# An output projection in 128-row tiles, fourteen products for fifteen, and four steps that move with it

## The chip, the core and the metric

The kernel runs on one core of a Trainium2 chip. A core has five engines with a queue of instructions each: TensorE (matrix products; PE in the profile, PEld its weight loads), VectorE (DVE), ScalarE (ACT), GpSimd (POOL) and SyncE (SP), which here issues every DMA. An engine works through its queue in order, and an instruction that waits holds up all behind it. The metric is device time in microseconds, lower is better.

## The reference

Two branches read the same normalized input and are multiplied. S = 2048 rows, D = 576 columns, H = 32 heads of 18 columns, F = 4608 hidden columns, all in fp32.

```python
xn  = layernorm(x)
qkv = xn @ wqkv                                  # three of 32 heads x 18
p   = softmax(einsum("bhqd,bhkd->bhqk", q, k) * 18 ** -0.5)
s   = einsum("bhqk,bhkd->bhqd", p, v).reshape(S, D) @ wo
g   = silu((gelu(xn @ w_gate) * (xn @ w_up)) @ w_down)
out = x + s * g
```

The change touches the product with `wo`, and the last line.

## The kernel before

**Split operands.** Where a product has to be more exact than one pass of TensorE's fp32r format, each operand is split into a high part (the value rounded to fp32r) and a low part (the rest), and three products are summed in PSUM: high with high, high with low, low with high. `split` does it on POOL (lines 93 to 96: one instruction for the high part, one for the low), `split_av` on ACT and VectorE, `split_ap` on ACT and POOL.

**The stages.** A prologue (lines 138 to 349) normalizes x, transposes it and makes q, k and v, all of which go to DRAM. It also splits `wo` into rows of `wos` in DRAM (`split_wo`, `store_wo`). Then the gated network (FFN) and the attention run together. The FFN is cut into 144 sections: each computes 128 hidden columns for a block of 512 rows (`section`, 54 matmuls into pg and pu), and its activation runs on ACT and VectorE (`activate`, lines 379 to 394) with one buffer t1, which `finish` then splits into hh and hl. After every second section four groups of six products go through w_down (`down`, py), and VectorE adds them to Y (line 412). The weights of a section are split by POOL in three chunks (wh, wl: five buffers each).

Nine sections come before the attention proper (`FIRST`, lines 756 to 773). They carry the first score products whose row maxima VectorE takes (`max_mm`, line 654). When one unit's maxima are complete, `max_neg` negates and splits them (three VectorE instructions), `max_end` transposes them with a matmul (line 667) and a DMA writes them beside q as extra rows. Then 128 sections (lines 774 to 795) run with the attention of 32 units, a unit being four heads and 512 rows: scores, Exp on ACT, and the product with v into acc. Seven sections close the FFN (lines 811 to 823), and lines 826 to 853 are the end.

**The output projection.** A unit's output goes to DRAM (oT), its sums' reciprocals too (rT). For each block of 512 rows, tiles of seven heads (126 rows; the fifth has four heads, 72 rows) are loaded into OT, with rT spread over a head's 18 rows in den (`load_o`, two DMAs a tile). `norm_o` multiplies them on POOL. den has one buffer. For each of eight groups of a block (128 rows × 288 columns) `split_o` splits OT into oh and ol on POOL, and `project_o` sums 15 products in PSUM (line 550). In the first three blocks VectorE multiplies by the gate (line 552), POOL adds x (line 553) and a DMA writes the rows. In the last block six groups are kept in S2 until the FFN is done. Then `gate` (ACT's Tanh and a VectorE instruction, line 377), a VectorE product (line 847) and POOL's addition of x (`put`, line 835) follow for each of them; the last two groups are projected at the very end (lines 849 to 853) and added on VectorE.

**What sets the order.** TensorE's instructions run in the order of the code. The other queues are ordered by a planner before the run: it takes the earliest ready instruction in the code's order, so that an instruction can come ahead of its place where its queue has room. `keep_in_program_order` holds single ones in place. `at(n, part, ...)` hangs a step to a part of section n, counted from the first attention section. Tiles of a later stage lie where tiles of the prologue were, and wait for them one by one. OT, with its zero fill on POOL (line 490), lies over the prologue's vn tiles; the KS tiles, whose fills of ones are shared by VectorE and POOL (line 605), lie over other tiles.

Of the kernel before, what the change touches and what calls it, by code (L numbers as in the profile page):

```python
# [17 lines left out]
P = 128  # L18
NT = S // P
TB = 512  # L20
# [20 lines left out]
FIRST = (0, 0, 4, 6, 6, 6, 6, 6, 6)  # L41
ATT = range(len(FIRST), len(FIRST) + NU * NA)
MROW = 3 * DH
HO = 7
KO = HO * DH
NK = -(-D // KO)
EPS = 1e-5
GC = 0.044715
GS = 0.7978845608028654
# [18 lines left out]
def kernel(ctx: ExitStack, tc: tile.TileContext, x, wqkv, wo, w_gate, w_up, w_down, out):  # L68
# [69 lines left out]
    with tc.tile_pool(name="pro", bufs=1) as pro, tc.tile_pool(name="pps", bufs=1, space=PSUM) as pps:  # L138
# [140 lines left out]
            nc.sync.dma_start(vs[t * P:(t + 1) * P, c * H // 2:(c + 1) * H // 2, :], v)  # L279

        def split_wo(k):
            n = min(KO, D - k * KO)
            raw = raw_tile([KO, D])
            tc.keep_in_program_order(nc.sync.dma_start(raw[0:n], wo[k * KO:k * KO + n, :]))
            hi, lo = (pro.tile([KO, D], F32R, name=f"wo{i}", tag="rawp", bufs=5) for i in range(2))
            split(hi[0:n], lo[0:n], raw[0:n])
            return k, n, hi, lo

        def store_wo(k, n, hi, lo):
            for i, t in enumerate((hi, lo)):  # L290
                tc.keep_in_program_order(nc.sync.dma_start(wos[i, k * KO:k * KO + n, :], f(t)[0:n]))

        NQT = 2 * D // P
        def after(what, before):
# [101 lines left out]
    def down(b, r, hs, wd, Y, js):  # L396
        for j in js:
            tt = slice(j * P, (j + 1) * P)
            for c in range(2):
                cc = slice(288 * c, 288 * c + 288)  # L400
                py = ps.tile([P, 288], F32, name="py", tag="s", bufs=2)
                n = 0
                for g in range(G):
                    hh, hl = hs[g]
                    for a, w in ((hh, wd[0]), (hh, wd[1]), (hl, wd[0])):
                        nc.tensor.matmul(py, a[:, tt], w[:, g, cc], start=(n == 0), stop=(n == 3 * G - 1))  # L406
                        n += 1
                yy = Y[:, j, cc]
                if r == 0:
                    nc.vector.tensor_copy(yy, py)  # L410
                else:
                    nc.vector.tensor_tensor(yy, py, yy, op=ALU.add)  # L412
# [73 lines left out]


    op = ctx.enter_context(tc.tile_pool(name="op", bufs=1, reuse_waits="tile"))
    OT = op.tile([KO, NK, TB], F32, name="OT")
    nc.gpsimd.memset(OT, 0.0)  # L490
# [12 lines left out]

    def norm_o(k):
        n, den = OG.pop(("den", k))
        nc.gpsimd.tensor_tensor(OT[0:n, k, :], OT[0:n, k, :], den[0:n], op=ALU.mult)
# [33 lines left out]
    def project_o(b, i, S2=None, o=None):  # L540
        c, j = divmod(i, TB // P)
        cc = place(b, i)[1]
        if b < NB - 1:
            xx, yy = OG["xy"]
        po = ps.tile([P, TB], F32, name="po", tag="m", bufs=3)
        o = o or OG["o"]
        terms = [(k, x, w) for k in range(NK) for x, w in ((0, 0), (0, 1), (1, 0))]
        for m, (k, x, w) in enumerate(terms):
            n = min(KO, D - k * KO)
            nc.tensor.matmul(po[:, 0:288], o[x][0:n, k, :], OW[w][0:n, k, :], start=(m == 0), stop=(m == len(terms) - 1))  # L550
        if b < NB - 1:
            nc.vector.scalar_tensor_tensor(yy, yy, 0.25, po[:, 0:288], op0=ALU.mult, op1=ALU.mult)
            nc.gpsimd.tensor_tensor(yy, yy, xx, op=ALU.add)
            OG["y", b, i] = yy
        elif S2 is not None:
            nc.scalar.activation(S2[:, j, cc], po[:, 0:288], AF.Copy)
        return po[:, 0:288]
# [13 lines left out]
            t()  # L571

    S2 = [None]
    for b in range(NB):
        last = b == NB - 1
        for k in range(NK):
            t0 = b * AB + max(-(-min(H, (k + 1) * HO) // QD) * NA + 3, 22 + 3 * k)
            if not (last and k == NK - 1):
                at(t0, 0, load_o, b, k)
                at(t0 + 2 - last, 2, norm_o, k)  # L580
        first = (b + 1) * AB + 1 if last else max((b + 1) * AB + 6, (b + 1) * NR * G - len(FIRST) + 3)
        if not last:
            first += (first + len(FIRST)) % G
# [16 lines left out]
    with tc.tile_pool(name="att", bufs=1, reuse_waits="tile") as att:  # L600
# [173 lines left out]
        for n in range(NU * NA):  # L774
# [23 lines left out]
    with tc.tile_pool(name="epi", bufs=1, reuse_waits="tile") as epi:  # L798
        S2[0] = epi.tile([P, TB // P, D], F32, name="S2")
        XX = epi.tile([P, TB // P, D], F32, name="XX")  # L800
        n = NU * NA
        todo[n, 2].insert(0, lambda: norm_o(NK - 1))
        def cut(hi, lo, raw):
            split_av(hi, lo, raw, tc.keep_in_program_order)

# [33 lines left out]
        for Y, j, c in finals:  # L839
            cc = slice(288 * c, 288 * c + 288)  # L840
            th = epi.tile([P, 288], F32, name="thl", bufs=len(finals))
            ss = S2[0][:, j, cc]
            gate(th, th, Y[:, j, cc])
            if c * (TB // P) + j > HIND:
                late[c * (TB // P) + j] = th, ss, j, cc
            else:
                nc.vector.scalar_tensor_tensor(ss, th, 0.25, ss, op0=ALU.mult, op1=ALU.mult)
# [34 lines left out]
```

## Time and profile before

| what | value |
|---|---|
| median of three runs | 2657.7 us (2654.64 to 2658.63) |
| profiled execution, own time | 2656.42 us |
| span of its instructions | 2654.6 us |
| mean granted TensorE clock | 0.998 of full |
| busy: PE, PEld, DVE, ACT, POOL | 99%, 77%, 75%, 57%, 52% |
| products of the output projection (line 550) | 480 (384 of 126 rows, 96 of 72 rows) |
| DMA issues of OT and den | 20 and 20 |

An instruction line of a timeline reads: start in us, duration in us, engine, source line, operation, written tile, read tiles, shapes, and in brackets the idle time before it with what ended it. Lines of a list by groups give the count (x128), busy us, mean ns of one, and idle time before with the releasers. A line of the stages has, for a stretch of time, its length, the busy time and the count of each engine, and last the granted clock, the busy share of the DMA engines and GB/s. Matmuls overlap in the record: the time that one costs is its distance from the next one's start.

### The profile page before, as it was taken

How to read it: one execution, taken by the hardware profiler on the slowest of the kernel's cores; microseconds unless marked ns; L12 is line 12 of the kernel's file. 1: busy time of each engine (PE TensorE's matmuls, PEld its weight loads, DVE VectorE, ACT ScalarE, POOL GpSimd, SP SyncE). 2: the span in 40 equal slices, each digit the busy share in tenths (PEclk: the TensorE clock that was granted, in tenths of full speed). 3: DMA queues.
4: the chain of work that ended last, by engine and by line, in shares of the span. 5: the costliest groups of instructions: out<-in, count | busy, mean ns of one | idle time of the engine just before them, and what ended most of it. 6: DMA issues, size and time to landing. Idle time of an engine off the chain costs nothing.

```text
span 2654.6 us, 55995 instructions
## 1 busy us (share of the span) xinstructions
PE 2639.3 (99%) x21032; PEld 2050.3 (77%) x21032; DVE 1999.4 (75%) x3440; ACT 1506.3 (57%) x2690; POOL 1392.4 (52%) x1488
## 2 busy tenths in 40 slices
PE   9999999999999999999999999999999999999999
PEld 8887777777777777777777777777777777777788
DVE  5327888888887888777888887778888877788445
ACT  3222466666666666555666665556666655566632
POOL 2126544545466555555447655555446755555564
PEclk9999999999999999999999999999999999999999
DMA  8875433334355434444346444435335444444341
GB/s 259 267 239 140 114 99 102 97 103 103 96 126 135 106 99 107 122 114 120 103 110 146 124 102 106 119 101 134 102 100 126 134 115 122 108 111 119 77 108 60
DMA packets 390874, 323.66 MB, mean 122 GB/s; under 512 B 105736, under 2 KB 305928, under 8 KB 390604
## 3 DMA queue, kind: packets, MB, share of 16 engines
q1 hardware_dynamic: 390604, 320.08, 45.3%
q8 instruction: 167, 2.74, 0.5%
q14 instruction: 103, 0.84, 0.1%
HBM read 266.58 MB, written 52.85 MB: 120 GB/s over the span
## 4 chain that ended last, share of the span: by engine, by line
PE 97%; POOL 1%; DVE 1%; DMA 0%; issue 0%; ACT 0%; SPq 0%; POOLq 0%; DVEq 0%
PE pg L369 27%; PE py L406 18%; PE acc L718 17%; PE pe L684 10%; PE pm L653 9%; PE pu L369 7%; PE po L159 7%; PE po L550 2%; PE po L212 0%; PE pt L221 0%; POOL wl L95 0%; PE pm L667 0%; DMA den<-rT 0%; DVE thl L377 0%; DMA vs<-vn 0%
## 5 line engine op out<-in xcount | busy, mean ns | idle before, releaser
L685 ACT ACTIVATE pT<-pe 128x512 f32<-128x512 f32 x2048 | 1165.2, 598 | 703.7 <-PE pm L653 533.5
L654 DVE TENSOR_REDUCE mx<-pm 128x1 f32<-128x512 f32 x2048 | 1289.1, 684 | 52.8 <-PE pm L653 32.2
L369 PE MATMUL pg<-xd,wh 64*128 64x512 f32 x2592 | 949.3, 398 | 0.5 <-issue 0.5
L369 PE MATMUL pu<-xd,wh 64*128 64x512 f32 x2592 | 948.9, 398 | 0.0
L684 PE MATMUL pe<-q,KS 56*128 56x512 f32 x2048 | 816.9, 406 | 0.0
L653 PE MATMUL pm<-KS,q 54*128 54x512 f32 x2048 | 796.5, 395 | 4.0 <-DVE mx L654 4.0
L369 PEld LDWEIGHTS pg<-xd,wh 64*128 64x128 f32 x2592 | 483.5, 187 | 66.3 <-issue 31.8
L94 POOL TENSOR_SCALAR wh<-raw 128x384 fp32r<-128x384 f32 x432 | 226.6, 525 | 557.0 <-PE pu L369 336.7
L369 PE MATMUL pg<-xd,wl 64*128 64x512 f32 x1296 | 508.1, 392 | 0.4 <-POOL wl L95 0.4
L369 PE MATMUL pu<-xd,wl 64*128 64x512 f32 x1296 | 508.0, 392 | 0.0
L369 PEld LDWEIGHTS pu<-xd,wh 64*128 64x128 f32 x2592 | 484.4, 187 | 6.2 <-DVE t L387 0.2
L718 PE MATMUL acc<-pT,VS 128*32 128x512 f32 x4096 | 466.0, 595 | 0.0
L95 POOL TENSOR_TENSOR wl<-raw,wh 128x384 fp32r<-128x384 f32 x432 | 440.5, 1021 | 34.3
L684 PEld LDWEIGHTS pe<-q,KS 56*128 56x128 f32 x2048 | 370.6, 184 | 80.9 <-ACT pT L685 20.5
L653 PEld LDWEIGHTS pm<-KS,q 54*128 54x128 f32 x2048 | 377.0, 185 | 30.1 <-DVE mx L654 6.4
L412 DVE TENSOR_TENSOR Y<-py,Y 128x288 f32<-128x288 f32 x544 | 248.4, 457 | 188.6 <-PE py L406 187.6
L406 PE MATMUL py<-dh,hh 128*128 128x288 f32 x1152 | 352.8, 306 | 1.8 <-DVE Y L410 1.6
L406 PE MATMUL py<-dl,hh 128*128 128x288 f32 x1152 | 339.6, 295 | 0.0
L406 PE MATMUL py<-dh,hl 128*128 128x288 f32 x1152 | 338.6, 294 | 0.0
L718 PEld LDWEIGHTS acc<-pT,VS 128*32 128x32 f32 x4096 | 120.3, 109 | 276.8 <-issue 265.0
L369 PEld LDWEIGHTS pg<-xd,wl 64*128 64x128 f32 x1296 | 242.5, 187 | 18.7 <-POOL wl L95 0.8
L406 PEld LDWEIGHTS py<-dh,hh 128*128 128x128 f32 x1152 | 215.8, 187 | 44.4 <-issue 37.7
(118 smaller groups left out, 2929.6 us busy)
## 6 DMA issues: line engine op xcount, KB each, us to landing
KS<-qk SPq DMA_DIRECT2D x1536, 36.0 KB
raw<-in_B_w_gate_dram SPq DMA_DIRECT2D x144, 288.0 KB
raw<-in_B_w_up_dram SPq DMA_DIRECT2D x144, 288.0 KB
raw<-in_B_w_down_dram SPq DMA_DIRECT2D x68, 576.0 KB
VS<-vs SPq DMA_DIRECT2D x128, 152.0 KB
qk<-t SPq DMA_DIRECT2D x72, 256.0 KB
q<-qk SPq DMA_DIRECT2D x384, 36.0 KB
xd<-xhs SPq DMA_DIRECT2D x24, 384.0 KB
```

Of the source, the lines that this page charges most:

```text
L94: first = nc.gpsimd.tensor_scalar(hi, raw, 1.0, 1.0, op0=ALU.mult, op1=ALU.mult)
L95: nc.gpsimd.tensor_tensor(lo, raw, f(hi), op=ALU.subtract)
L159: nc.tensor.matmul(o, st, m, start=(i == 0), stop=(i == len(TERMS) - 1))
L369: nc.tensor.matmul(o, w[1 + wp][k][rr, c, :], xd[xp][k][rr, c, :], start=(i == 0), stop=(i == len(terms) - 1))
L406: nc.tensor.matmul(py, a[:, tt], w[:, g, cc], start=(n == 0), stop=(n == 3 * G - 1))
L412: nc.vector.tensor_tensor(yy, py, yy, op=ALU.add)
L550: nc.tensor.matmul(po[:, 0:288], o[x][0:n, k, :], OW[w][0:n, k, :], start=(m == 0), stop=(m == len(terms) - 1))
L653: nc.tensor.matmul(pm, QS[u, r][rr, t * P:(t + 1) * P], KS[(u * NA + c) % KB][r][rr, :], start=True, stop=True)
L654: nc.vector.tensor_reduce(MX[u][:, 2 * r + a, t, c:c + 1], pm, axis=AX.X, op=ALU.max)
L684: nc.tensor.matmul(pe, KS[(u * NA + c) % KB][r][rr, t * P:(t + 1) * P], QS[u, r][rr, :], start=True, stop=True)
L685: nc.scalar.activation(PT[u, kt][:, 2 * r + a, :], pe, AF.Exp, scale=SCALE)
L718: nc.tensor.matmul(ACC[u][32 * a:32 * a + 32, :], VS[(u * NA + c) % VB][:, v:v + 32], pt[:, a, :], start=(kt == 0), stop=(kt == NT - 1), s ...
```

## The change

The 576 rows of `wo` and of OT are now cut by 128: four tiles and a fifth of 64 rows. The low part of the fifth tile is copied under its high part (`oh` rows 64 to 127, a POOL copy in `split_o`), and `woh` holds the fifth tile's rows twice, `wol` once with zeros under it. Two products of full height then do what three did, and a group has fourteen. Heads straddle tiles, so `load_o` issues a DMA for each run of whole heads or part of a head: 13 for OT and 13 for den in a block. The tiles woh and wol are allocated once.

Four things move. The zero fill of OT, with that of wol's last rows, stands in the code at attention section 4 and no longer ahead of the KS fills. `max_neg` of the first unit comes before the activation of its section and no longer after. The normalizations of tiles 3 and 4 come one section after their loads; in the last block tile 3 is loaded in two parts (heads up to 27, and head 28 after the last unit), and both tiles are normalized after it. In the last `down` the second half of the columns takes its PSUM buffers from the tag "f", so that py has four buffers and not two. At the end VectorE and no longer POOL adds x for the six groups.

```diff
-HO = 7
-KO = HO * DH
-NK = -(-D // KO)
+NK = KT + 1
...
-                py = ps.tile([P, 288], F32, name="py", tag="s", bufs=2)
+                py = ps.tile([P, 288], F32, name="py", tag="sf"[c if b == NB - 1 and r == NR - 1 else 0], bufs=2)
...
-    OT = op.tile([KO, NK, TB], F32, name="OT")
-    nc.gpsimd.memset(OT, 0.0)
-    OW, OG = {}, {}
-
-    def load_o(b, k, pool=op):
-
-        h0, h1 = k * HO, min(H, (k + 1) * HO)
-        n = (h1 - h0) * DH
+    OT = op.tile([P, NK, TB], F32, name="OT")
+    OW = [op.tile([P, NK, 288], F32R, name=name) for name in ("woh", "wol")]
+    OG = {}
+
+    def load_o(b, k, pool=op, heads=range(H)):
+
         toks = slice(b * TB, (b + 1) * TB)
-        den = pool.tile([KO, TB], F32, name="den")
-        nc.sync.dma_start(OT[0:n, k, :], oT.rearrange("g (a p) t -> (g a) p t", p=32)[h0:h1, 1:DH + 1, toks])
-        nc.sync.dma_start(den[0:n], rT[h0:h1, toks].rearrange("h (o s) -> h o s", o=1)
-                          .to_broadcast([h1 - h0, DH, TB]))
-        OG["den", k] = n, den
+        if ("den", k) not in OG:
+            OG["den", k] = pool.tile([P, TB], F32, name="den")
+        den = OG["den", k]
+        row, end = k * P, min(D, (k + 1) * P)
+        while row < end:
+            h, d = divmod(row, DH)
+            m = max(1, (end - row) // DH) if d == 0 else 1
+            e = min(DH, d + end - row)
+            n = m * (e - d)
+            rows = slice(row - k * P, row - k * P + n)
+            row += n
+            if h in heads:
+                nc.sync.dma_start(OT[rows, k, :], oT.rearrange("g (a p) t -> (g a) p t", p=32)[h:h + m, 1 + d:1 + e, toks])
+                nc.sync.dma_start(den[rows], rT[h:h + m, toks].rearrange("h (o s) -> h o s", o=1)
+                                  .to_broadcast([m, e - d, TB]))
...
     def load_wo(c):
-        for i, name in enumerate(("woh", "wol")):
-            w = OW[i] = op.tile([KO, NK, 288], F32R, name=name)
+        for i, w in enumerate(OW):
             cc = slice(288 * c, 288 * c + 288)
-            m = (NK - 1) * KO
-            nc.sync.dma_start(f(w)[:, 0:NK - 1, :], wos[i, 0:m, cc].rearrange("(k p) n -> p k n", p=KO))
-            nc.sync.dma_start(f(w)[0:D - m, NK - 1, :], wos[i, m:D, cc])
+            nc.sync.dma_start(f(w)[:, 0:KT, :], wos[i, 0:R0, cc].rearrange("(k p) n -> p k n", p=P))
+            for a in range(2 - i):
+                nc.sync.dma_start(f(w)[HR * a:HR * a + HR, KT, :], wos[i, R0:D, cc])
...
-        oh, ol = (pool.tile([KO, NK, P], F32R, name=m) for m in ("oh", "ol"))
+        oh, ol = (pool.tile([P, NK, P], F32R, name=m) for m in ("oh", "ol"))
         split(oh, ol, OT[:, :, j * P:(j + 1) * P])
+        nc.gpsimd.tensor_copy(oh[HR:P, KT, :], ol[0:HR, KT, :])
...
-        terms = [(k, x, w) for k in range(NK) for x, w in ((0, 0), (0, 1), (1, 0))]
+        terms = [(k, x, w) for k in range(KT) for x, w in ((0, 0), (0, 1), (1, 0))] + [(KT, 0, 0), (KT, 0, 1)]
...
+    LATE = range(H - QD), range(H - QD, H)
     for b in range(NB):
         last = b == NB - 1
         for k in range(NK):
-            t0 = b * AB + max(-(-min(H, (k + 1) * HO) // QD) * NA + 3, 22 + 3 * k)
-            if not (last and k == NK - 1):
+            t0 = b * AB + max(-(-min(D, (k + 1) * P) // (QD * DH)) * NA + 3, 22 + 3 * k)
+            if last and k == KT - 1:
+                at(NU * NA - 1, 0, load_o, b, k, op, LATE[0])
+            if not last or k < KT - 1:
+                t0 += k == KT
                 at(t0, 0, load_o, b, k)
-                at(t0 + 2 - last, 2, norm_o, k)
+                at(*((t0 + 2 - last, 2) if k < KT - 1 else (t0 + 1, 0)), norm_o, k)
...
-            section((n == 2) * 4 * none + [lambda s=s: lead_pair(s) for s in range(slot, slot + m)] + (m > 0) * none,
+            end = [lambda: max_neg(0, tc.keep_in_program_order)] if slot + m >= NS > slot else none
+            section((n == 2) * 4 * none + [lambda s=s: lead_pair(s) for s in range(slot, slot + m)] + (m > 0) * end,
...
-            if slot >= NS > slot - m:
-                max_neg(0, tc.keep_in_program_order)
...
+            if n == NA:
+                nc.gpsimd.memset(OT, 0.0)
+                nc.gpsimd.memset(f(OW[1])[HR:P, KT, :], 0.0)
...
-        todo[n, 2].insert(0, lambda: norm_o(NK - 1))
+        for k in (KT, KT - 1):
+            todo[n, 2].insert(0, lambda k=k: norm_o(k))
...
-                load_o(NB - 1, NK - 1, epi)
+                load_o(NB - 1, KT - 1, op, LATE[1])
+                load_o(NB - 1, KT, epi)
...
-                put(ss, j, cc, nc.gpsimd)
+                put(ss, j, cc, nc.vector)
```

More of the change, by code (lines that the diff above doesn't have):

```diff
@@ L281, in split_wo @@
         def split_wo(k):
[L282 to L285, printed above, removed]
+            n = min(P, D - k * P)
+            raw = raw_tile([P, D])
+            tc.keep_in_program_order(nc.sync.dma_start(raw[0:n], wo[k * P:k * P + n, :]))
+            hi, lo = (pro.tile([P, D], F32R, name=f"wo{i}", tag="rawp", bufs=5) for i in range(2))
             split(hi[0:n], lo[0:n], raw[0:n])
@@ L290, in store_wo @@
             for i, t in enumerate((hi, lo)):
-                tc.keep_in_program_order(nc.sync.dma_start(wos[i, k * KO:k * KO + n, :], f(t)[0:n]))
+                tc.keep_in_program_order(nc.sync.dma_start(wos[i, k * P:k * P + n, :], f(t)[0:n]))
         NQT = 2 * D // P
@@ L504, in norm_o @@
     def norm_o(k):
-        n, den = OG.pop(("den", k))
-        nc.gpsimd.tensor_tensor(OT[0:n, k, :], OT[0:n, k, :], den[0:n], op=ALU.mult)
+        n = min(P, D - k * P)
+        nc.gpsimd.tensor_tensor(OT[0:n, k, :], OT[0:n, k, :], OG.pop(("den", k))[0:n], op=ALU.mult)
     def load_wo(c):
-        for i, name in enumerate(("woh", "wol")):
-            w = OW[i] = op.tile([KO, NK, 288], F32R, name=name)
+        for i, w in enumerate(OW):
             cc = slice(288 * c, 288 * c + 288)
-            m = (NK - 1) * KO
-            nc.sync.dma_start(f(w)[:, 0:NK - 1, :], wos[i, 0:m, cc].rearrange("(k p) n -> p k n", p=KO))
-            nc.sync.dma_start(f(w)[0:D - m, NK - 1, :], wos[i, m:D, cc])
+            nc.sync.dma_start(f(w)[:, 0:KT, :], wos[i, 0:R0, cc].rearrange("(k p) n -> p k n", p=P))
+            for a in range(2 - i):
+                nc.sync.dma_start(f(w)[HR * a:HR * a + HR, KT, :], wos[i, R0:D, cc])
@@ L546, in project_o @@
         o = o or OG["o"]
-        terms = [(k, x, w) for k in range(NK) for x, w in ((0, 0), (0, 1), (1, 0))]
+        terms = [(k, x, w) for k in range(KT) for x, w in ((0, 0), (0, 1), (1, 0))] + [(KT, 0, 0), (KT, 0, 1)]
         for m, (k, x, w) in enumerate(terms):
-            n = min(KO, D - k * KO)
-            nc.tensor.matmul(po[:, 0:288], o[x][0:n, k, :], OW[w][0:n, k, :], start=(m == 0), stop=(m == len(terms) - 1))
+            nc.tensor.matmul(po[:, 0:288], o[x][:, k, :], OW[w][:, k, :], start=(m == 0), stop=(m == len(terms) - 1))
         if b < NB - 1:
```

## The prediction, made before the change was run

> **What bounds the kernel now.** I read the page first: busy shares, then the chain that ended last.
>
> ```profile
> PE 2639.3 (99%) x21032; PEld 2050.3 (77%) x21032; DVE 1999.4 (75%) x3440; ACT 1506.3 (57%) x2690; POOL 1392.4 (52%) x1488
> ...
> PE 97%; POOL 1%; DVE 1%; DMA 0%; issue 0%; ACT 0%; SPq 0%; POOLq 0%; DVEq 0%
> ```
>
> TensorE carries the chain nearly everywhere, so a matmul saved should be time saved, if TensorE really runs at its own pace there. The groups by shape say what one lasts (mean ns) and how long the engine idled before it.
>
> ```profile
> L550 PE MATMUL po<-woh,ol 126*128 126x288 f32 x128 | 37.6, 293 | 0.0
> ...
> L550 PE MATMUL po<-woh,ol 72*128 72x288 f32 x32 | 9.4, 294 | 0.0
> ```
>
> Products of 72 and 126 rows last the same, and so do py's of 128 rows (L406, 294). In the same list POOL's weight splits idle 557.0 us, 336.7 of it until TensorE releases a buffer (pu, L369): POOL is the one that is ahead. Matmuls overlap, so the price is their spacing, from the timeline of PE near the end:
>
> ```profile
> 2601.07 0.29 PE L550 MATMUL po<-woh,oh 72*128 72x288 f32 x1
> 2601.21 0.29 PE L550 MATMUL po<-wol,oh 72*128 72x288 f32 x1
> ```
>
> Spacing 0.13 us (fifteen start from 2599.49 to 2601.34, 0.132 each). The remaining 3% of the chain lies at two ends. First the passage from the projections to the attention: POOL's timeline, then a line each of ACT's, DVE's and PE's.
>
> ```profile
> 201.82 2.24 POOL L490 MEMSET OT<- 126x2560 f32 x1 [6.25 <-DMA KS<-qk]
> 204.00 2.87 POOL L605 MEMSET KS<- 128x512 f32 x6
> ...
> 213.56 1.29 POOL L100 TENSOR_TENSOR hl<-t,hh 128x512 fp32r<-128x512 f32 x1
> ```
>
> ```profile
> 214.88 0.60 ACT L382 ACTIVATE t<-pg 128x512 f32<-128x512 f32 x1 [5.22 <-POOL hl L100]
> 218.26 2.48 DVE L654 TENSOR_REDUCE mx<-pm 128x1 f32<-128x512 f32 x4
> 219.00 0.79 PE L653 MATMUL pm<-KS,q 54*128 54x512 f32 x1 [4.03 <-DVE mx L654]
> ```
>
> POOL stands still until 201.82 for the zero fill of OT; the fills of KS, the weight splits and hl queue behind it. hl's input hh was ready at 209.66 (ACT, 209.03 and 0.63), hl ended at 214.85, ACT's Square needs the one t1 buffer that hl reads, VectorE's reduces stand behind that activation, and TensorE idles 4.03 us. The stages show what follows, the granted clock being the third value from the right:
>
> ```profile
> 219.00:225.00 6.00, 6.00 (x28) 4.58 (x29) 4.31 (x7) 1.54 (x3) 5.92 (x6) 0.57 0.88 222
> ...
> 280.00:300.00 20.00, 18.81 (x144) 15.83 (x144) 17.89 (x36) 5.63 (x9) 11.53 (x12) 1.00 0.53 149
> ```
>
> After that gap the clock is 0.57 for 6 us; the 1.19 us gap at 287.25 (TensorE waiting for the negated maxima) left it at 1.00. Second, the very end, where VectorE carries the chain:
>
> ```profile
> 2643.73 0.44 DVE L847 SCALAR_TENSOR_TENSOR S<-thl,S 128x288 f32<-128x288 f32 x1
> 2644.09 0.44 DVE L412 TENSOR_TENSOR Y<-py,Y 128x288 f32<-128x288 f32 x1
> 2644.46 0.91 DVE L377 SCALAR_TENSOR_TENSOR thl<-thl,Y 128x288 f32<-128x288 f32 x1
> ```
>
> ```profile
> 2644.25 0.81 POOL L835 TENSOR_TENSOR S<-S,XX 128x288 f32<-128x288 f32 x1 [1.13 <-DVE S L847]
> ```
>
> VectorE's steps take 0.37 us from start to start, but thl takes 0.91 whenever POOL's addition runs beside it (0.45 when none does).
>
> **Part by part.**
>
> *Fourteen products for fifteen.* 32 groups lose one each. The 24 of the first three blocks and six of the last lie on TensorE's path: 30 × 0.131 = −3.9 us. The last two feed the VectorE-bound end and give nothing. Full height costs nothing by the rows above. Ends: −3.0 (a quarter hidden by some other wait) to −4.2.
>
> *Zero filling later.* POOL has nothing to do between 195.6 and 201.8 but wait for this fill's buffers, so the six KS fills (2.87) start about 195.6 instead of 204.0; VectorE's own KS fills, eight of the same kind, ran at 183.4 to 188.9, so their memory is free. The first split after them then waits for TensorE's release near 199.6, and hl for its own input at 209.66. Wherever the fill (2.24) lands between, that slack of over 5 us covers it, and later POOL's lead does. hl and all behind it move 3.9 us (213.56 to 209.66). TensorE's gap falls to about 1 us, which the 1.19 us row says costs no clock; then the eight reduces that took 218.26 to 224.14 run at 0.61 each, 4.9 in place of 5.9: another −1.0. I take −4.5, keeping back 0.4 because the weights of the section after were only issued by SP at 214.44. Ends: 0 (POOL's other work fills the hole) and −6.3 (3.9 plus 2.4, what 5.25 us at about half clock lose). The small fill of wol (64 rows × 288, under a KS fill's 0.53) lies under the same cover.
> [...]
>
> *Maxima negated earlier.* TensorE's matmul at 287.25 waited 1.19 us for three small VectorE steps (0.21, 0.16, 0.17) that came behind an activation and four additions. Put ahead of the activation, they delay its first step (283.09) by about 0.4 and the first additions that free PSUM likewise. −1.0; ends −0.4 and −1.3. No DMA moves: the row copies into q stay behind the matmul and start earlier with it.
>
> *End: four PSUM buffers, additions on VectorE.* TensorE's 48 last py products ran 2637.27 to 2644.75, 7.48 us where 48 × 0.131 = 6.29: 1.2 us of waiting for two buffers goes, but off the path, as VectorE is late. VectorE started 26 instructions between 2638.26 and 2651.12 (ended 2651.58). With six more: 32 × 0.37 = 11.8, plus 0.45 of first waits, plus 0.1 where an addition directly follows its producer (2650.65 to 2651.12 is 0.47), about half of eight: 12.7 against 13.3. −0.5; ends −1.1 (none of these) and +2.8 (six more at 0.47 and the slow thl stay).
>
> *Loads by 128 rows.* Heads now straddle tiles: 13 OT and 13 den DMAs a block for 5 and 5, 64 more in all, and 8 more for the doubled wo rows. Issues took 0.35 (KS) to 0.82 (den): 25 to 59 us of SP over the whole time, where SP's waits on POOL's splits alone are 393.4 us. The normalizations of tiles 3 and 4 now come one section after their loads, and POOL's queue stands behind their wait. Before, POOL waited for den 15 times, 8.8 us at most, and once 10.0 for a weight; TensorE waited 0.4 us for wl in the sections. Two or three more issues of 0.82 per normalization stay under that: 0. The 32 copies of the low part, between 0.13 (an eighth of 64×1536's 1.50) and 0.29 (identity's 128×128), are 4 to 9 us on an engine with 48% free: 0.
> Only after the last head, where POOL starts at 2565.75 when den lands, is the cover thin (POOL, then PE):
>
> ```profile
> 2573.93 2.01 POOL L95 TENSOR_TENSOR wl<-raw,wh 128x384 fp32r<-128x384 f32 x2
> ```
>
> ```profile
> 2578.02 0.39 PE L369 MATMUL pg<-xd,wl 64*128 64x512 f32 x1
> ```
>
> The first wl of the pair is ready at 2574.96, 3.0 us ahead of its use. Ahead of it POOL gets a second normalization (1.29), two later den issues (2 × 0.63) and two copies (0.3 to 0.6): 2.9 to 3.2. +0.3; ends 0 and +3.0, if pieces land apart or splits reorder.
> [...]
>
> Sum: −3.9 − 4.5 − 1.0 − 0.5 + 0.3 = −9.6. The profiled execution took 2656.42 (span 2654.6 and 1.8 around): 2646.8. The median, 2657.7, is 1.3 higher, so for a median 2648.1; I say **2648**.
>
> **The rivals.** *The hole is not used:* the fill, or other POOL work, takes the old place, and the first passage gives 0. For it: each queue's order is planned ahead of time and the plan put the fill there once. Against: the KS fills come first in the code now. −5.1, 2652.6. *Slower, by POOL's queue:* a normalization that waits for late pieces holds up the weight splits at the ends of the blocks. It decides once a wait exceeds POOL's lead, over the 10.0 us shown to be harmless; each us above costs one. To be slower by 5 it must cost 15 in all, some 5 in each of the first three, so waits of 15 us where 8.8 was the longest: 2663. *The end grows:* thl is slow for another reason and six additions cost 0.47 each: −6.3, 2651.4. *No gain from the matmuls:* another engine sets the sections; VectorE's 75% and 0.4 us of TensorE idleness speak against: −5.7, 2652.
>
> **How the numbers follow.** Forecast 0.62, unused hole 0.15, slower 0.10, end grows 0.08, no gain 0.05. A measurement can tell about 0.2% (5.3 us) from no change. Below 2652.4: the forecast but for a little, the grown end, half of the two near 2652.5: 0.78. Same 0.12, slower 0.10. The likeliest case alone spans 2644.8 (all terms at their best, −12.9) to 2652. The range, **2643 to 2655**, adds 2 us of scatter (runs: 2654.64 to 2658.63) and the cases near 2652.5.
>
> **What would show it.** Right: po in 448 products at 0.13 spacing; KS fills on POOL before 200; TensorE idle before pm near 215 about 1 us and the clock at 1.00 there; no wait of over 0.5 before the first negated-maxima matmul; thl near 0.45 at the end, VectorE done 12 to 13 us after its first Y. Wrong: POOL's fill of OT still at 201.8, wl as TensorE's releaser at the block ends or after the last head, or thl still at 0.9.

## The result, and the profile after

The changed kernel takes 2646.43 us (median of six runs, 2645.63 to 2648.32) against 2656.71 for the kernel before on the same chip: a ratio of 0.9965, interval 0.9955 to 0.9975. That is 10.3 us less (6.6 to 12.0 by the interval); the forecast was 2648, from a sum of -9.6. Of the 1.6 between forecast and result, 1.0 is the median of the kernel before, which was 2657.7 over three runs and is 2656.71 over six. The profiled execution took 2646.48 us, its span 2644.2, against 2656.42 and 2654.6.

First the page after, the engines' busy times and the chain that ended last:

```profile
PE 2633.0 (100%) x21000; PEld 2046.0 (77%) x21000; DVE 2002.0 (76%) x3446; ACT 1506.2 (57%) x2690; POOL 1396.9 (53%) x1515
...
PE 97%; DVE 1%; POOL 0%; DMA 0%; ACT 0%; issue 0%; SPq 0%; POOLq 0%; DVEq 0%
```

TensorE still carries 97% of the chain. It runs 32 instructions fewer (21000 for 21032), one for each group of the output projection, and POOL's 1% of the chain is gone.

The rest is read stage by stage. Below, a "shift" is the difference of two traces in the time at which a section of the FFN begins (its first matmul into pg), both counted from the start of the first section. So what the prologue scatters (up to 1.1 us between the traces) is left out.

| stretch | forecast | shift in the trace, us |
|---|---|---|
| zero filling later (first to fourth section) | -4.5 | -5.28 |
| maxima negated earlier (ninth section) | -1.0 | -1.14 |
| products, up to the last section | part of -3.9 | -3.44 |
| three changes of block (-0.97, -0.88, +1.67), steps of 0.4 to 0.5 elsewhere | 0 | +0.46 |
| start of the last section | | -9.40 |
| last section to VectorE's last instruction | -0.5 and the last products | -0.60 |
| from there to the span's end | | -0.45 |

Together -10.45. The "products" row holds 28 steps of 0.114 on average (-3.19), one at each section that holds a group but for one whose step of -0.50 is in the row below it, and -0.26 of smaller steps at the other sections (single ones up to 0.16).

**The passage into the attention.** POOL's timeline of the changed kernel, then a line each of ACT's, DVE's and PE's (start, duration, in brackets the idle time ahead and what ended it):

```profile
196.21 2.86 POOL L614 MEMSET KS<- 128x512 f32 x6
199.89 0.51 POOL L92 TENSOR_SCALAR wh<-raw 128x384 fp32r<-128x384 f32 x1 [0.82 <-PE pu L367]
200.34 2.24 POOL L793 MEMSET OT<- 128x2560 f32 x1
...
210.09 1.29 POOL L98 TENSOR_TENSOR hl<-t,hh 128x512 fp32r<-128x512 f32 x1 [1.29 <-ACT hh L97]
```

```profile
211.41 0.60 ACT L380 ACTIVATE t<-pg 128x512 f32<-128x512 f32 x1 [1.40 <-POOL hl L98]
214.80 4.87 DVE L663 TENSOR_REDUCE mx<-pm 128x1 f32<-128x512 f32 x8
215.53 0.50 PE L662 MATMUL pm<-KS,q 54*128 54x512 f32 x1 [1.27 <-DVE mx L663]
```

The six KS fills start at 196.21 in place of 204.00. The planner put OT's fill at 200.34, ahead of its place in the code and into the middle of a weight split; by then its memory is free and it waits for nothing, so nothing stands behind such a wait here. POOL now waits for hl's input, not hl for POOL: hl starts at 210.09 where it started at 213.56, and TensorE waits 1.27 us where it waited 4.03. The eight reduces take 4.87 us without an interruption, and behind the gap the clock (third value from the right) stays full:

```profile
215.50:221.50 6.00, 5.96 (x40) 4.35 (x41) 5.46 (x10) 2.62 (x5) 5.74 (x5) 1.00 1.08 224
```

**TensorE's waits** between the first sections and the last, of the kernel before (total us, times, longest):

```profile
PE pm L653 <- DVE mx L654: 4.0, 1, 4.0
PE py L406 <- DVE Y L410: 1.6, 2, 0.8
PE pm L667 <- DVE m L662: 1.2, 1, 1.2
PE pg L369 <- POOL wl L95: 0.4, 1, 0.4
```

and of the changed kernel:

```profile
PE py L404 <- DVE Y L408: 1.4, 1, 1.4
PE pm L662 <- DVE mx L663: 1.3, 1, 1.3
```

The wait for the negated maxima is gone. So are two waits of py at changes of block (near 818 and 1458), and one has come at the third (2088.5); no part of the sum had spoken of these.

**The products and the end.** The first products of a group near the end (PE's timeline), and some of VectorE's last instructions (DVE's):

```profile
2590.49 0.29 PE L555 MATMUL po<-woh,oh 128*128 128x288 f32 x1
2590.62 0.29 PE L555 MATMUL po<-wol,oh 128*128 128x288 f32 x1
```

```profile
2638.51 0.81 DVE L375 SCALAR_TENSOR_TENSOR thl<-thl,Y 128x288 f32<-128x288 f32 x2
...
2640.71 0.44 DVE L865 SCALAR_TENSOR_TENSOR S<-thl,po 128x288 f32<-128x288 f32 x1
2641.19 0.46 DVE L848 TENSOR_TENSOR S<-S,XX 128x288 f32<-128x288 f32 x1
```

Products of full height keep the spacing of 0.13. At the end two thl take 0.81 together; before, 1.43. VectorE goes from its first Y (2628.82) to its end (2641.65) in 12.83 us with 32 instructions, before in 13.32 with 26.

### The profile page after: what moved, and what is told of

Its sections match the earlier page's. It is cut to its first block, busy times and chain, and to the rows that moved or that the text cites. A ratio compares the mean times of both kernels' runs of the same rounds, so it can differ in the third digit from the quotient of the medians.

```text
span 2644.2 us, 56069 instructions
## 1 busy us (share of the span) xinstructions
PE 2633.0 (100%) x21000; PEld 2046.0 (77%) x21000; DVE 2002.0 (76%) x3446; ACT 1506.2 (57%) x2690; POOL 1396.9 (53%) x1515
## 4 chain that ended last, share of the span: by engine, by line
PE 97%; DVE 1%; POOL 0%; DMA 0%; ACT 0%; issue 0%; SPq 0%; POOLq 0%; DVEq 0%
PE pg L367 27%; PE py L404 18%; PE acc L727 17%; PE pe L693 10%; PE pm L662 9%; PE pu L367 7%; PE po L157 6%; PE po L555 2%; PE po L210 0%; PE pt L219 0%; DVE mx L663 0%; DMA xd<-xhs 0%; PE pm L676 0%; DMA raw<-in_B_w_up_dram 0%; DVE Y L410 0%
```

## The experiments

Each is the changed kernel with one edit unless it says "before". Times are set against runs of the kernel before on the same chip. Differences between two variants compare medians from different chips; those below some 1 us are read from the traces, which show one execution of each.

**1. Before, with OT's fill on VectorE**

```
-    nc.gpsimd.memset(OT, 0.0)
+    nc.vector.memset(OT, 0.0)
```

> The kernel before with one word changed: the zero fill of OT is VectorE's and no longer POOL's, at its old place in the code; nothing else of the change. Theory (POOL's queue stands behind a fill that waits for the prologue's last stores, and hl, the activation, the reduces and TensorE stand behind POOL): VectorE waits in its place, where it has nothing to do from 189 to 204, so POOL fills KS before 200, hl starts near 210, TensorE's gap before pm shrinks from 4.0 us to about 1.3, the clock stays at 1.00, and the fourth section starts 4.5 to 5.3 us earlier: 2651 to 2652.5 beside 2656.7. Rival (the passage is limited by the fill itself, by a DMA or by ACT, whoever does it): the gap stays at 4 us, no change, 2656.7. Second rival (VectorE's fill now holds up the first activation): the gap shrinks by less than 2 us.

Measured: 2655.67 us against 2655.71, ratio 1.0001 (0.9992 to 1.001). The theory's time did not come; the second rival comes nearest, since the gap shrank by 0.37. VectorE's timeline of this kernel shows why, with POOL's hl:

```profile
202.87 2.19 DVE L490 MEMSET OT<- 126x2560 f32 x1 [18.54 <-DMA vs<-vn]
205.11 4.27 DVE L605 MEMSET KS<- 128x512 f32 x8
...
209.36 0.67 DVE L383 SCALAR_TENSOR_TENSOR t<-t,pg 128x512 f32<-128x512 f32 x1
```

```profile
214.07 1.28 POOL L100 TENSOR_TENSOR hl<-t,hh 128x512 fp32r<-128x512 f32 x1 [5.58 <-ACT hh L99]
```

The fill only changed queues. On VectorE it waits for the same memory until 202.87, and VectorE's own eight KS fills, which had run at 183 to 189 in the kernel before, now stand behind it. The first step of the activation starts at 209.36, where it started at 204.46 before, and hl, now waiting 5.58 us for its input, starts at 214.07. TensorE's gap stays at 4.05 from start to start (4.42 before). The passage gained 1.25 us all the same (0.59 of it ahead of the gap, where wl now came in time), and in this trace sections further on lost 2.3, above all at two changes of block (+0.81 and +0.73).

**2. Both zero fills put back ahead of the KS fills**

```
+    nc.gpsimd.memset(OT, 0.0)
+    nc.gpsimd.memset(f(OW[1])[HR:P, KT, :], 0.0)
...
-            if n == NA:
-                nc.gpsimd.memset(OT, 0.0)
-                nc.gpsimd.memset(f(OW[1])[HR:P, KT, :], 0.0)
```

> The changed kernel with both zero fills put back ahead of the KS fills on POOL. Theory: the whole loss of the passage comes back, a gap of about 4 us before pm, clock near 0.57 for 5 to 6 us after it, and the fourth section 4.5 to 5.3 us later: 2651 to 2652. Rival (the passage got better because the tiles of the projection lie elsewhere and wait for other stores): under 1.5 us comes back, 2646.5 to 2648.

Measured: 2649.41 us, ratio 0.9974 (0.9964 to 0.9984): 3.0 above the changed kernel (2.4 by the ratios), less than expected. POOL's timeline, and the clock behind the gap:

```profile
200.63 2.24 POOL L490 MEMSET OT<- 128x2560 f32 x1 [3.81 <-DMA vs<-vn]
...
212.88 1.29 POOL L98 TENSOR_TENSOR hl<-t,hh 128x512 fp32r<-128x512 f32 x1
```

```profile
218.30:224.30 6.00, 5.97 (x26) 4.24 (x26) 4.34 (x7) 1.47 (x3) 5.89 (x6) 0.50 1.09 258
```

The wait, the queue behind it and the slow clock are back: a gap of 3.47 and 0.50 for 6 us. In the trace the passage is 3.83 worse than in the changed kernel, and still 1.45 better than before.

That OT lies elsewhere in memory is not shown to be the reason. By the semaphores in the traces, the fill waits in both kernels for the same stores of the prologue (vs<-vn). The bracket of the kernel before names KS<-qk, whose transfers use some of the same semaphores. In the traces the semaphore of such a store rises in 16 steps. For the last of these stores, 15 steps had come 1.8 us after its issue in every trace. The sixteenth came by 2.0 us in ten of the 14 traces, and only at 3.6 to 4.2 us in four (1.84 in the changed kernel, 4.21 in the kernel before): the kernel before and run 1, with OT in its old place, and runs 9 and 11, with OT in its new one. The kernel before was profiled in an execution with a late store. So the fill's place in the queue is worth 3.83 with the store in time, and the 1.45 is put down to the late store, though no run separates it.

**3. Before, with OT's fill alone put later**

```
-    nc.gpsimd.memset(OT, 0.0)
...
+            if n == NA:
+                nc.gpsimd.memset(OT, 0.0)
```

> The kernel before with one edit: the zero fill of OT is issued by POOL in the second section, behind the fills of KS, as in the changed kernel; nothing else is changed (fifteen products, the old loads and end). The fill on VectorE had failed, since VectorE's own fills of KS stood behind it. Theory (POOL's queue alone made the gap): hl starts within 1.5 us of its input, the gap before pm falls from 4.42 to 1.4 to 1.9, the clock stays at 1.00 behind it, the section to follow starts 4.0 to 5.5 us earlier than in the kernel before; time 2651 to 2653. Rival (the loads by 128 rows or the new order of the queues did it): the gap stays above 3 and the clock near half, 2655 to 2657.

Measured: 2652.70 us against 2656.17, ratio 0.9989 (0.9979 to 0.9998). POOL's timeline and the windows around the gap:

```profile
200.88 2.24 POOL L784 MEMSET OT<- 126x2560 f32 x1
...
210.10 1.29 POOL L100 TENSOR_TENSOR hl<-t,hh 128x512 fp32r<-128x512 f32 x1 [1.29 <-ACT hh L99]
```

```profile
209.55:215.55 6.00, 5.25 (x47) 4.82 (x44) 2.72 (x5) 2.81 (x6) 1.29 (x1) 1.00 0.44 150
215.55:221.55 6.00, 5.99 (x40) 4.39 (x41) 5.46 (x10) 2.63 (x5) 5.88 (x6) 1.00 1.07 219
```

With fifteen products and all else as before, hl starts at 210.10, the gap is 1.14 and the clock stays full; the fourth section starts 5.8 us earlier by the shift, both a little beyond the expected (1.4 to 1.9, and 4.0 to 5.5). This one line makes the whole gain of the passage, with OT in its old place in memory. By the last section of this trace 4.35 is left, and in the medians 3.5 (2.9 by the ratio, 0.5 to 5.6 by its interval): part of it went in steps of 0.4 at sections 25, 53 and 85. Steps of that size sit at other sections in every trace, so they are taken as scatter.

**4. Nineteen products for fourteen**

```
-        terms = [...] + [(KT, 0, 0), (KT, 0, 1)]
+        terms = [...] + [(KT, 0, 0), (KT, 0, 1)] + [(k, 1, 1) for k in range(NK)]
```

> The changed kernel with five products more in each of the 32 groups (low part with low part for each tile, which adds next to nothing to the sum): 19 of full height for 14. Theory (TensorE paces every section that holds a group, 0.131 us a product): 30 groups on the path, 30 x 5 x 0.131 = 19.7 us, up to 21.0 with the last two: 2666 to 2667.5. Rival (sections have room that hides products): under 10 us, below 2657.

Measured: 2665.31 us, ratio 1.0035 (1.0022 to 1.0048): 18.9 us above the changed kernel (18.6 by the ratios), 0.7 under the expected stretch. In the trace the sections that hold a group fall behind by 0.55 to 0.72 each (once 0.94), mostly 0.6 to 0.7, that is 0.13 for each of the five added products; 18.9 over 30 groups of five is 0.126. A product on TensorE's path cost its spacing here. VectorE's end grew by only 0.38 where TensorE's last product came 2.08 later: there products are hidden, as forecast.

**5. The first maxima negated late again**

```
-            ... + (m > 0) * end,
+            ... + (m > 0) * none,
...
+            if slot >= NS > slot - m:
+                max_neg(0, tc.keep_in_program_order)
```

> The changed kernel with the negation of the first unit's maxima put back behind the activation. Theory: TensorE waits again about 1.2 us before the matmul on the negated maxima, all behind it 1.0 to 1.2 us later: 2647.5. Rival (the gain of this step was the passage's, further ahead, and not its own): no wait of over 0.5 us there, 2646.4.

Measured: 2647.98 us, ratio 0.9966 (0.9953 to 0.9979), 1.5 above the changed kernel's median, which the scatter does not tell from 1.1. TensorE's waits of this kernel:

```profile
PE pm L676 <- DVE m L671: 1.2, 1, 1.2
PE py L404 <- DVE Y L408: 0.5, 1, 0.5
```

The wait of 1.2 is back, and the ninth section starts 1.14 later than in the changed kernel: the term by itself. The second line shows the other thing that moves: the wait of py at the third change of block is 0.5 where the changed kernel has 1.4, and by the last section this trace is 0.81 ahead of it.

**6 and 7. The end taken apart.** One edit gives the six additions back to POOL, the other gives py two PSUM buffers again:

```
-                put(ss, j, cc, nc.vector)
+                put(ss, j, cc, nc.gpsimd)
```

> The changed kernel with one edit: the last six additions of x (one per group of the last unfinished tiles) go back to POOL; the four PSUM buffers and everything else stay. In the changed kernel VectorE went from its first sum of the end (Y) to its last instruction in 12.83 us, in the kernel before in 13.32. Theory of the prediction (the products thl are slow because POOL adds beside them): thl lasts 0.8 to 0.9 again in four or five places, and the stretch is 13.0 to 13.6 although VectorE has six instructions fewer; 0.2 to 0.8 us slower than the changed kernel. Rival (POOL's additions cost nothing, the gain came from the PSUM buffers): six instructions of 0.37 fewer and no slow thl, 10.6 us, 2 us faster.

```
-                py = ps.tile(..., tag="sf"[c if b == NB - 1 and r == NR - 1 else 0], bufs=2)
+                py = ps.tile(..., tag="s", bufs=2)
```

> The changed kernel with one edit: the last py products get two PSUM buffers again in place of four; the additions stay on VectorE. In the changed kernel the 48 last py products ran in 6.23 us, in the kernel before in 7.48, and VectorE needed 12.83 from its first Y to its end. Theory of the prediction (TensorE waits 1.2 us for two buffers, but off the path, as VectorE is late): the py products take 7.3 to 7.6 again, VectorE 12.7 to 13.0, the time within 0.3 us of the changed kernel. Rival (VectorE lives on the earlier py): VectorE takes 13.3 to 14 and the whole 0.5 to 1.2 us more.

Measured: 2647.92 us (ratio 0.9969, 0.9959 to 0.9979) and 2647.09 (0.9969, 0.9957 to 0.9981), 1.5 and 0.7 above the changed kernel's median, inside the scatter. DVE's and POOL's timelines with the additions on POOL:

```profile
2639.28 1.41 DVE L375 SCALAR_TENSOR_TENSOR thl<-thl,Y 128x288 f32<-128x288 f32 x2
```

```profile
2639.44 0.94 POOL L848 TENSOR_TENSOR S<-S,XX 128x288 f32<-128x288 f32 x1 [0.77 <-DVE S L860]
```

thl beside POOL's addition is slow again, four times (0.91 to 1.06; the line above holds one of 1.04), and a product S once (0.69). VectorE needs 12.96 us for 26 instructions, 0.13 more than for 32 without POOL, and the span ends 3.47 us after VectorE instead of 2.60: 1.0 us in all, 0.87 of it behind VectorE's end. With two buffers py's stretch is 6.94 us (6.24 with four), under the 7.3 to 7.6 expected, and VectorE's 13.12: 0.3 more. So of the -0.49 to VectorE's end, the four buffers give about 0.3 and the additions 0.13; the 0.45 behind it goes with the additions, though this tail scatters too (2.60 in most variants, 2.90 in runs 11 and 12). The buffers were expected to lie off the path and lie a little on it.

**8. The half tile's normalization one section later**

```
-                at(*((t0 + 2 - last, 2) if k < KT - 1 else (t0 + 1, 0)), norm_o, k)
+                at(*((t0 + 2 - last, 2) if k < KT - 1 else (t0 + 1 + (k == KT), 0)), norm_o, k)
```

> The changed kernel with one edit: the normalization of the half tile (64 rows) of each block comes one section later, so that in POOL's queue it no longer stands ahead of the gates' products and of the split hl at the block's change. In the changed kernel TensorE waits 1.4 us there at 2088.5 for VectorE's copy Y, which comes behind hl. Theory (the small form of the rival by POOL's queue: the normalization and its 3.07 us of waiting for den make hl late): the wait at 2088.5 is gone, 1.0 to 1.5 us faster than the changed kernel in the trace. Rival (POOL waited 1.50 us for TensorE behind that normalization, so it was early enough): the wait stays at 1 to 1.7 us.

Measured: 2646.73 us, ratio 0.9966 (0.9953 to 0.9979). Inconclusive: the planner left POOL's order as it was, with the normalization at the same place, and the stall stayed at 1.73 from start to start. So the next run leaves the instruction out.

**9. Without that normalization**

```
-        nc.gpsimd.tensor_tensor(OT[0:n, k, :], OT[0:n, k, :], OG.pop(("den", k))[0:n], op=ALU.mult)
+        den = OG.pop(("den", k))
+        if k < KT:
+            nc.gpsimd.tensor_tensor(OT[0:n, k, :], OT[0:n, k, :], den[0:n], op=ALU.mult)
```

> The changed kernel without POOL's normalization of the half tile of 64 rows (four instructions of 1.29; the last head's output stays unnormalized, so that part of the computation is left out). The edit of its due time had left POOL's order as it was. Theory (that normalization, waiting 2.6 to 3.1 us for den, makes hl late at the third change of block): the stall of TensorE near 2088 (1.3 to 1.7 from start to start) is gone. Rival (the splits behind it wait for TensorE anyway, 1.39 to 1.50 us in the traces): the stall stays at 1.2 to 1.8 and the whole is within 1 us of the changed kernel.

Measured: 2646.88 us in one run. POOL's timeline of the changed kernel at the third change of block, with ACT's line:

```profile
2073.49 1.28 POOL L512 TENSOR_TENSOR OT<-OT,den 64x512 f32<-64x512 f32 x1 [3.07 <-DMA den<-rT]
2076.27 0.51 POOL L92 TENSOR_SCALAR wh<-raw 128x384 fp32r<-128x384 f32 x1 [1.50 <-PE pe L693]
...
2084.78 1.28 POOL L93 TENSOR_TENSOR hl<-t,hh 128x512 fp32r<-128x512 f32 x1
...
2086.09 0.60 ACT L380 ACTIVATE t<-pg 128x512 f32<-128x512 f32 x1 [2.30 <-POOL hl L93]
```

and without the normalization:

```profile
2076.26 0.51 POOL L92 TENSOR_SCALAR wh<-raw 128x384 fp32r<-128x384 f32 x1 [5.28 <-PE pu L367]
...
2084.77 1.28 POOL L93 TENSOR_TENSOR hl<-t,hh 128x512 fp32r<-128x512 f32 x1
```

hl starts at the same time with the normalization and without it, though TensorE comes 0.9 later to this place in run 9: counted from the start of the section (2072.93 and 2073.81), hl is 0.88 earlier there, and the wait of py fell from 1.4 to 0.6, below what the rival expected. The variants that keep the normalization show waits from 0.4 to 1.4 here, so this does not tell it from scatter. What the split behind it waits for does. The bracket names TensorE, whose semaphore rises 33 times between 2066 and 2076 in the changed kernel's trace. The split also waits for the two DMAs that load its weights (raw), and the semaphore of the second rises 0.17 or 0.18 us before the split starts, at the second and third change of block in all 14 traces. The normalization ends 0.8 to 1.6 us ahead of the split and is cleared, and the theory with it.

The load of the weights is late because of SP's queue. SP's timeline of the changed kernel, then SP's and POOL's of the kernel before:

```profile
2068.33 1.57 SPq L507 DMA_DIRECT2D den<-rT  x2
2070.00 0.66 SPq L111 DMA_DIRECT2D raw<-in_B_w_gate_dram  x1
```

```profile
2077.13 0.62 SPq L113 DMA_DIRECT2D raw<-in_B_w_gate_dram  x1
2083.52 0.51 POOL L94 TENSOR_SCALAR wh<-raw 128x384 fp32r<-128x384 f32 x1 [5.04 <-DMA raw<-in_B_w_up_dram]
```

The load takes the buffer that POOL's split dl leaves, at 2068.85 here and at 2076.91 before. Here the two den issues of the half tile stand ahead of it. It is issued 1.13 to 1.16 us after dl in the eleven kernels with the new loads, and 0.03 to 0.22 us after it in the three with the old ones. Run 9 kept these issues. TensorE's wait for py at this change is 0.4 to 1.4 us in the eleven and 0 to 0.5 in the three. At the first change it is the other way round: 0.2 to 0.9 us with the old loads and none with the new. At the second it comes and goes with both (0.8 to 1.6 us in five traces, none in nine). No edit of the den issues was tried, so their price of about 1 us at the third change is read from traces and not from an experiment.

**10. Score maxima three steps later in the third section**

```
-            section((n == 2) * 4 * none + ...
+            section((n == 2) * 7 * none + ...
```

> The changed kernel with one edit: in the third section of the attention the first two pairs of maxima come three steps later, so that TensorE's matmuls pm, which wait 1.3 us there for VectorE's maxima, come behind more of the gate's matmuls. Theory (the 1.3 us is a matter of order on TensorE's queue, the weights being there): the gap at 213.9 falls to 0.3 to 0.8 us and the section to follow starts 0.5 to 1.0 earlier. Rival (TensorE has nothing else to do until the activation behind hl has freed its buffers): the gap moves to another matmul and stays at 1.1 to 1.7.

Measured: 2647.08 us, ratio 0.9966 (0.9953 to 0.9979). PE's timeline:

```profile
215.90 0.50 PE L662 MATMUL pm<-KS,q 54*128 54x512 f32 x1 [0.58 <-DVE mx L663]
```

The wait fell from 1.27 to 0.58, as the theory had it, and the next section starts when it did (shift -0.03). TensorE reaches the next pm pairs early and waits for the reduces there (the four matmuls pm that follow start 0.60 apart, as the reduces do): VectorE's eight reduces, not TensorE's order, set this stretch. So the remaining gap is no longer a cost by itself, and no version came out of these runs that beats the changed kernel measurably.

**11 and 12. Only the gap made longer**, by repeating the first hl subtraction on POOL once, or twice with range(2):

```
+        if n == 0:
+            for _ in range(1):
+                nc.gpsimd.tensor_tensor(hl, FF["act"], f(hh), op=ALU.subtract)
```

> The changed kernel with one more POOL subtraction of the first hl (the same result written once more, 1.29 us), so that TensorE's gap before pm grows from 1.66 to about 2.95 from start to start. Theory (the clock falls only behind a gap that is longer, as the 3.47 of the kernel with both fills back): the clock stays at 1.00 behind it and the next section starts 1.2 to 1.4 later than in the changed kernel. Rival (any gap beyond some 2 us costs half a clock for 3 to 7 us): the clock in the 6 us behind is 0.5 to 0.8 and the section starts 2.5 to 4 later.

> The changed kernel with two more POOL subtractions of the first hl (2.58 us), so that the gap before pm is about 4.2 from start to start, nearly the 4.42 of the kernel before. Theory: the clock falls to 0.5 to 0.75 for the 6 us behind, as in the kernel before (0.57) and in the one with the fill on VectorE (0.72), and the next section starts 4 to 5.5 later than in the changed kernel, which gives back the whole gain of the passage with nothing changed but the gap. Rival (the clock fell for another reason, such as the DMA traffic there): it stays at 1.00 and only 2.6 are lost.

Measured, one run each: 2646.36 and 2648.97 us. The windows behind the gap, first with one more subtraction:

```profile
217.37:223.37 6.00, 6.00 (x40) 4.35 (x41) 5.44 (x10) 2.62 (x5) 5.91 (x6) 1.00 1.09 253
```

then with two:

```profile
218.56:224.56 6.00, 6.00 (x35) 4.81 (x36) 5.06 (x9) 1.69 (x4) 5.91 (x6) 0.73 0.80 205
```

A gap of 3.05 kept the full clock and cost 1.41, its own length more than the 1.66. A gap of 4.39 lost the clock and cost 3.57: 2.73 for the gap and 0.84 for the clock. That is less than the 4 to 5.5 expected: the clock is 0.73 in the 6 us behind this gap, where the kernel before has 0.57 behind one of 4.42 (last section). The gap's length and the clock behind it are thus shown to be most of the passage's loss, 3.57 of 5.28; where the rest comes from, these two runs do not show.

## Why the prediction was right, point by point

- *Zero filling later, -4.5:* right in mechanism, and the cause is shown by runs 2 and 3. The parts: 0.75 ahead of the gap (the 0.4 us wait of pg for wl went too, which the forecast had not counted), 2.76 for the gap (4.42 to 1.66 from start to start), and 1.77 behind it, from the clock and the reduces. The steps in the forecast were off singly: hl moved by 3.5, not 3.9, as VectorE's step ahead of it took 1.53 us beside a POOL split in place of 1.24; TensorE's wait fell to 1.27 and not "about 1"; the reduces took 4.87, the 4.9 forecast. The forecast took the wait until 201.82 as given, but it was that of an execution with a late store: 1.45 of the -5.28 are put down to it. In the medians runs 2 and 3 put the fill's place at 3.0 and 3.5.
- *The hole is not used* (15%): it fell. The planner did hoist the fill, but behind the KS fills and into time in which POOL had slack.
- *Fourteen products, -3.9:* 28 steps of -0.114 are -3.19; at this price 30 groups give -3.4, and run 4 gives 0.126 to 0.136 for one product. This is inside the stated ends, a little under the sum. *No gain from the matmuls* fell with it.
- *Maxima, -1.0:* -1.14; the delay of the activation's first step, feared to give some back, does not show.
- *The end, -0.5:* -0.49 to VectorE's end (12.83 against a forecast 12.7), plus 0.45 behind it that the sum lacked; run 6, which hands the additions back, has 0.87 there. The share of the PSUM buffers was put at nothing and is 0.3. *The end grows* fell: thl takes 0.44 as soon as POOL is quiet; the one that still takes 0.87 runs beside POOL's last split.
- *After the last head, +0.3:* 0. The two normalizations end at 2559.93 and the first wl of the pair at 2568.1; TensorE waits nowhere in the closing sections, so the end of +3.0, for pieces that land apart, did not come either; no run shows such a price.
- *Loads and copies, 0:* wrong for the loads at one place. The forecast set 25 to 59 us of issues against 393.4 us of SP's waiting over the whole run, and at the third change of block two of the issues stand ahead of an urgent load: about 1 us (run 9). The 32 copies of the low part took 0.33 us on average, above the 0.13 to 0.29 given (0.13 is a twelfth of 1.50, not an eighth), on an engine that has room.
- *Slower, by POOL's queue* (10%): near in place, wrong in price and in cause. A normalization does wait (3.07 us), but its successor waits longer, for the load of its weights, which stands behind den's issues on SP. The changes of block gave -0.97, -0.88 and +1.67; that term was missing from the sum, and that it nearly cancels is luck, since the -0.88 comes and goes with either kind of load. The step of -0.50 near 2286 stands at the same place in all eleven kernels with the new loads (with the added products taken off in run 4) and in none of the others. It was not explained.

The whole, -10.3 in the medians for -9.6, is closer than the single steps, and that is luck in part: in the traces the passage gained 0.8 more than forecast, with the help of a late store in the kernel before, and the output's end 0.45 more, while the products and the changes of block gave some 0.8 less.

## What to carry to other kernels

A cheap instruction that waits for memory, here a fill of 2.24 us, cost what stood behind it on its queue, and on another engine's queue it did so again (run 1: 2655.67 us for 2655.71); the same fill put later on the same queue brought the gain (run 3: 2652.70 for 2656.17). Look at what the waiting instruction heads, and move it behind the urgent work, not merely elsewhere. The same goes for the queue that issues DMAs: SP's 393.4 us of waiting over the whole run did not pay for two issues ahead of an urgent load, which went out 1.13 to 1.16 us after its buffer was free and not 0.03 to 0.22. A wait in a profile is that of one execution, and what ended it is inferred: the fill's wait until 201.82 was longer than in most traces, and a bracket named the wrong transfer there and the wrong engine in run 9. Gains of a few us in one stage arrived here (-5.28 in the passage), but short waits elsewhere shifted by about 1 us (-0.97, -0.88 and +1.67 at the changes of block), so small terms are proven in the stage's own rows and not in the whole time.

## What the runs showed of the hardware that was not expected

The clock did not follow the length of the gap. The gap (start to start) in one trace of each kernel, and the mean granted clock of the 6 us behind it:

| kernel | gap, us | clock in the 6 us behind |
|---|---|---|
| changed | 1.66 | 1.00 |
| 9, no last normalization | 2.14 (214.36 to 216.50) | 0.72 |
| 11, one more subtraction | 3.05 (214.32 to 217.37) | 1.00 |
| 2, fills put back | 3.47 (214.86 to 218.33) | 0.50 |
| 1, fill on VectorE | 4.05 (215.46 to 219.51) | 0.72 |
| 12, two more | 4.39 (214.18 to 218.56) | 0.73 |
| before | 4.42 (214.58 to 219.00) | 0.57 |

The windows around the gap of 2.14 (clock third from the right): the full clock up to the gap's end, and 0.72 behind it, though TensorE is busy there for 5.99 of 6.00 us.

```profile
210.50:216.50 6.00, 4.25 (x37) 3.82 (x34) 2.72 (x5) 2.33 (x5) 1.85 (x2) 1.00 0.48 161
216.50:222.50 6.00, 5.99 (x32) 4.18 (x33) 4.88 (x8) 1.67 (x3) 5.91 (x6) 0.72 1.12 248
```

In the kernel before, run 2 and run 12 the clock is down already in the 6 us ahead of the gap's end (0.86, 0.94 and 0.98). A gap of 2.14 lost the clock and one of 3.05 did not, so the length alone did not decide it; what did was not shown. Run 9's gap is longer than the changed kernel's because there the fill of OT waited for the late store after all (POOL's timeline of run 9):

```profile
202.20 2.24 POOL L795 MEMSET OT<- 128x2560 f32 x1 [1.32 <-DMA KS<-qk]
```

The 1.19 us row on which the forecast leaned was enough for the 1.66 of the changed kernel, but it does not vouch for longer gaps: in run 9 the clock fell behind one of 2.14.

The slow thl is the other observation: 0.44 or 0.45 us alone, 0.91 to 1.06 beside POOL's addition and 0.72 to 0.87 beside a POOL split, in the kernel before and again in run 6, which hands nothing but the additions back. VectorE ran 26 instructions with the additions beside it in 12.96 us, and 32 without them in 12.83.
